# Moving GpSimd's hold for one DMA transpose, and the load of q of batch 5, ahead of a spectrum sum

## The chip, the cores and the metric

The kernel runs on one core of a Trainium2 chip. The metric is the device time of one execution in microseconds, lower being better. The kernel before was timed three times: 216.16, 216.46 and 216.47 us, with a median of 216.46 us.

## The reference, cut to what matters

Two layers follow each other. The first is linear attention without a softmax over 8 batches of 8 heads, 576 rows and 64 columns; the second is a gated long convolution, done with a Fourier transform over the 576 rows.

```python
kv  = einsum('bhsd,bhse->bhde', k, v)
o   = einsum('bhsd,bhde->bhse', q, kv)
x   = o / sqrt(mean(o * o, -1) + 1e-6) * g_norm     # heads side by side: [8, 576, 512]
x1, x2, x3 = split(x @ w_proj, 3, axis=-1)
conv = irfft(rfft(x2, axis=1) * rfft(filter_fft, axis=0), n=576, axis=1)
out = (x1 * conv * x3) @ w_out                      # [8, 576, 512] in float32
```

## The kernel before, in words

The kernel goes through the eight batches as a hand-written software pipeline. The string `ORDER` (lines 20 to 53) lists steps as `name.batch`; the loop at the end of the kernel calls them in that order, and each step appends its instructions to the queues of the engines it uses. Each engine (PE, the matmul engine; DVE, VectorE; ACT, ScalarE; POOL, GpSimd; SP, SyncE, which only issues DMAs) works through its own queue strictly in that order. Between engines a framework adds the waits that the data need: a step that writes a buffer waits for those that read its old content and a step that reads waits for the writer. So a word of `ORDER` that is moved changes the place of its instructions in the queue of its own engine, and nothing else in the code.

The steps that matter here, with their lines in the kernel before:

- `Lq.b`, `Lk.b`, `Lv.b` (line 121): one DMA each, issued by POOL, that loads q, k or v of batch b from memory, turning float32 into bfloat16, into one of two buffers (`qb`, `kb`, `vb`; batch b uses buffer b modulo 2). `Lq.5` writes the q buffer that batch 3 used.
- `Qt.b` (line 409): a DMA transpose, issued by SP, from the q buffer into `qT`, again one of two. It waits for the landing of `Lq.b`. Batches 2 to 7 use it; batches 0 and 1 are transposed on PE.
- `Qh.b` (line 413): a POOL copy of two elements of `qT` into a tile that nobody reads. It waits for the landing of `Qt.b`, and so holds whatever comes behind it in POOL's queue until then. This is the hold of the title.
- `K.b` and `eK.b` (lines 384 and 390): k times v on PE, and its copy out of PSUM by ACT. `O01.b` and `O23.b` (line 458): q times that product for two groups of heads each, on PE; they need `qT`. `sq`, `ob`, `R`, `rs`, `x0`, `x1` (lines 468, 475, 465, 479, 493): square, copy, sum of squares, reciprocal root, and the normalised x.
- `fd`, `fr`, `fa` (lines 504 to 518): sums and differences of thirds of x ahead of the Fourier transform, on DVE. `F0`, `F1`, `F2`: forward transform on PE. `M0`, `M1` (line 606): products with the filter's spectrum on DVE, from PSUM into a float32 buffer. `M2` (line 621): the same for the small third group. `A0`, `A1` (line 612): the spectrum sums on POOL, which add two halves of that float32 buffer into `Y`. In batches 0 and 7 DVE does one of them (`Av1`).
- `Io01`, `I01`, `Io23`, `I23` (lines 658 and 659): the inverse transform on PE from `Y`. Line 659 multiplies the part that `A0` writes.
- `Ga`, `Gb` (line 631): the projections for x1 and x3 on PE. `x1` followed by a second digit, as in `x12.3` (line 637), and `g` (line 639): their evictions, the second with the product x1 times x3.
- `U`, `ot` (lines 754 to 774): the output product, its copy by ACT into one of three tiles, and four DMAs to memory issued by SP.

PSUM is four pairs of banks. A matmul group takes the pair that has been free longest, and is held by the step that still has to evict it.

POOL's queue around the change is, in the order before: `Lv.4`, `Qh.3`, `A1.2`, `Lk.5`, `Lv.5`, `A0.2`, `Lq.5`, `Lk.6`, `Qh.4`, `A1.3`, `Lv.6`, `A0.3`, `Lq.6`, `Qh.5`. SP's queue is: the DMAs of `ot0.0`, `Qt.4`, those of `ot2.0`, `ot0.1` and `ot4.1`, `Qt.5`, those of `ot2.1`, `Qt.6`, those of `ot0.2`.

Of the kernel before, what the change touches and what calls it, by code (L numbers as in the profile page):

```python
# [28 lines left out]
F1t.1 A0.1 Ga3.1 rs1.2 M1.1 K.3 Gb3.1 x13.1 x1.2 eK.3 F2.1 O23.3 g3.1 F2t.1 Lq.4 sq3.3 Lk.4 M2.1 A1.1 sq2.3 U0.0  # L29
Io01.1 ob3.3 I01.1 x0.2 ob2.3 os01.1 ot0.0 Ga2.1 Io23.1 fd.2 x12.1 Ga1.2 u01.1 os23.1 fa.2 x11.2 I23.1 R3.3 Gb2.1  # L30
rs3.3 O01.3 sq0.3 u23.1 g2.1 ob0.3 abM.2 R0.3 Ga0.2 w.1 sq1.3 Lv.4 fr.2 ob1.3 abT.2 rs0.3 x10.2 eT.2 R1.3 fin.1 Gb1.2
eab.2 rrM.2 rs1.3 F1.2 R2.3 F1t.2 g1.2 rrT.2 rs2.3 F2.2 err.2 x0.3 Qh.3 K.4 Qt.4 eK.4 F2t.2 M1.2 A1.2 U2.0 x1.3 M2.2
Ga3.2 O23.4 ot2.0 x13.2 sq3.4 fr.3 Lk.5 F0.2 U0.1 sq2.4 ob3.4 Gb3.2 ob2.4 Gb0.2 Lv.5 M0.2 A0.2 fd.3 ot0.1 rrM.3 R2.4
rrT.3 g0.2 Ga2.2 g3.2 rs2.4 R3.4 err.3 Io01.2 x12.2 I01.2 os01.2 rs3.4 U4.1 Io23.2 fa.3 Gb2.2 u01.2 os23.2 I23.2 abM.3
Lq.5 ot4.1 abT.3 g2.2 x1.4 u23.2 eab.3 w.2 Ga0.3 eT.3 F1.3 O01.4 F1t.3 x10.3 U2.1 Qt.5 sq1.4 ob1.4 sq0.4 M1.3 Lk.6
Ga1.3 ob0.4 fin.2 ot2.1 F0.3 R0.4 x11.3 rs0.4 Qh.4 K.5 eK.5 F2.3 M0.3 A1.3 Gb0.3 R1.4 g0.3 F2t.3 M2.3 rs1.4 Ga2.3
x12.3 Gb2.3 O23.5 g2.3 sq3.5 ob3.5 Gb1.3 x0.4 Lv.6 A0.3 Ga3.3 g1.3 Io01.3 sq2.5 Lq.6 ob2.5 os01.3 x13.3 I01.3 fd.4
fa.4 u01.3 fr.4 U0.2 Io23.3 Qt.6 ot0.2 abT.4 eT.4 os23.3 Gb3.3 g3.3 O01.5 I23.3 abM.4 sq0.5 u23.3 w.3 Ga0.4 sq1.5
ob0.5 R3.5 ob1.5 eab.4 x10.4 K.6 F2.4 R2.5 rs3.5 eK.6 F2t.4 rs2.5 Qh.5 fin.3 rrM.4 R1.5 M2.4 rs1.5 F1.4 R0.5 F1t.4
# [842 lines left out]
```

## Time and profile before

| what | value |
|---|---|
| median of three runs | 216.46 us |
| the profiled execution, its own time | 218.23 us |
| span from first to last instruction in that execution | 216.5 us |
| PE busy | 200.6 us, 93% of the span |
| DVE busy | 182.6 us, 84% |
| ACT busy | 147.9 us, 68% |
| POOL busy | 70.6 us, 33% |
| granted PE clock, mean | 0.994 |

All times below are microseconds from the start of the span, in one profiled execution. A row of a timeline gives the start, the duration, the engine, the line of the kernel, the operation, the tiles written and read, the shapes and a count; in brackets stands the time that the engine sat idle before it, and what ended that. `SPq` is SP's queue. A DMA has two times: the time that its issuing engine was occupied, and the time from issue to landing, which another view gives in a row that ends with that number. In the table of windows each engine's busy time in a stretch stands with its count of instructions, and at the end of the row are the granted clock, the busy share of the DMA engines (1.00 is sixteen engines with one packet each) and the rate in GB/s.

### The profile page before, as it was taken

To read this page: it belongs to the slowest core of one execution; us is meant where nothing else is said; L and a number is where in the kernel's file an instruction comes from. 1 tells how busy PE (TensorE), PEld (TensorE's weight loads), DVE (VectorE), ACT (ScalarE), POOL (GpSimd) and SP (SyncE) were. 2 spreads that over 40 slices of the span, in tenths; PEclk is the share of its full clock that TensorE was granted. 3 is DMA by queue.
4 is the path that set the end of the run, shared out by engine and by line. 5 is a ranking of instruction groups with operands and counts; after the bars stand their busy time and mean duration, and the time that the engine had idled before them with its cause. 6 is when DMAs were issued, how large, how long until landed. Compare 5 with 4: busy or idle time off the path is not lost.

```text
span 216.5 us, 4609 instructions
## 1 busy us (share of the span) xinstructions
PE 200.6 (93%) x1852; PEld 122.0 (56%) x1852; DVE 182.6 (84%) x275; ACT 147.9 (68%) x232; POOL 70.6 (33%) x67
## 2 busy tenths in 40 slices
PE   4879999999999999999879999999999999999960
PEld 1544555574657555665555566656574586557620
DVE  7875888799999999989869977899988899998830
ACT  3688775989959888659567978677666863524430
POOL 8662001404294007702910047107600440042031
PEclk9999999999999999999999999999999999999997
DMA  3999999999969944999996903999340221102584
GB/s 41 201 211 204 207 202 204 172 197 166 203 84 196 201 89 81 189 233 175 142 241 109 152 3 88 168 236 182 88 117 0 76 74 41 56 3 74 121 208 133
DMA packets 40810, 30.12 MB, mean 139 GB/s; under 512 B 15796, under 2 KB 36276, under 8 KB 40788
## 3 DMA queue, kind: packets, MB, share of 16 engines
q0 software_dynamic: 21376, 17.63, 53.0%
q1 hardware_dynamic: 19172, 11.80, 26.4%
q10 hardware_dynamic: 240, 0.39, 0.7%
q8 instruction: 14, 0.23, 0.4%
q14 instruction: 8, 0.07, 0.1%
HBM read 33.69 MB, written 9.44 MB: 199 GB/s over the span
## 4 chain that ended last, share of the span: by engine, by line
PE 64%; DMA 11%; issue 8%; POOL 5%; ACT 5%; DVE 4%; POOLq 0%; DVEq 0%; ACTq 0%
PE ps L631 23%; PE ps L754 9%; DMA wp<-in_moe_w_proj_dram 7%; PE ps L548 6%; PE ps L658 4%; DMA qT<-qb 4%; PE ps L554 2%; PE ps L465 2%; DVE tpw L606 2%; PE ps L534 2%; PE ps L384 2%; PE ps L458 2%; POOL kb L121 2%; PE ps L580 1%; PE ps L573 1%
## 5 line engine op out<-in xcount | busy, mean ns | idle before, releaser
L612 POOL TENSOR_TENSOR Y<-tpw 97x1024 bf16<-97x1024 f32 (+1 forms) x14 | 38.8, 2773 | 109.5 <-DVE tpw L606 109.4
L631 PE MATMUL ps<-x,wp 128*128 128x288 bf16 x512 | 71.3, 286 | 1.3 <-DMA wp<-in_moe_w_proj_dram 0.5
L631 PEld LDWEIGHTS <-wp 128*128 128x128 bf16 x512 | 48.5, 98 | 19.7 <-issue 3.3
L606 DVE TENSOR_TENSOR tpw<-ps,HH 97x2048 f32<-97x2048 f32 (+1 forms) x16 | 36.6, 2287 | 3.4 <-PE ps L587 1.8
L639 DVE TENSOR_TENSOR g<-ps,x 128x576 bf16<-128x576 f32 x32 | 23.9, 753 | 7.0 <-PE ps L631 4.8
L479 ACT ACTIVATE rstd<-ps,bias_eps 128x576 bf16<-128x576 f32 x32 | 23.3, 745 | 6.5 <-PE ps L465 6.3
L637 ACT CAST x<-ps 128x576 bf16<-128x576 f32 x32 | 20.5, 644 | 10.5 <-PE ps L631 10.3
L754 PE MATMUL ps<-wo,yg 128*128 128x512 bf16 x112 | 26.3, 379 | 0.0
L558 ACT CAST x<-ps 128x1024 bf16<-128x1024 f32 (+1 forms) x24 | 20.4, 881 | 6.8 <-PE ps L548 3.3
L468 ACT ACTIVATE sq<-ps 128x576 bf16<-128x576 f32 x32 | 20.2, 661 | 5.4 <-PE ps L458 5.3
L475 ACT ACTIVATE o<-ps,g_col 128x576 bf16<-128x576 f32 x28 | 20.5, 758 | 0.0
L758 ACT COPY ot<-ps 128x1024 f32<-128x1024 f32 x13 | 13.2, 1016 | 7.6 <-PE ps L754 7.6
L754 PEld LDWEIGHTS <-yg 128*128 128x128 bf16 x112 | 10.6, 98 | 11.6 <-issue 0.5
L658 PE MATMUL ps<-IV,Y 128*128 128x192 bf16 x120 | 15.5, 245 | 0.0
L548 PE MATMUL ps<-wp,ab 128*128 128x512 bf16 x64 | 15.1, 379 | 0.0
L662 ACT COPY os<-ps 128x576 f32<-128x576 f32 x15 | 9.6, 639 | 7.8 <-PE ps L659 4.7
L493 DVE TENSOR_TENSOR x<-o,rstd 128x1152 bf16<-128x1152 bf16 x16 | 12.0, 755 | 2.9 <-ACT rstd L479 2.9
L667 DVE TENSOR_TENSOR u<-ps,os 128x576 bf16<-128x576 f32 x15 | 11.3, 754 | 3.3 <-ACT os L662 1.7
L465 PE MATMUL ps<-sq,ind 128*128 128x288 bf16 x64 | 12.8, 286 | 0.4 <-ACT kvblk L390 0.3
L659 PE MATMUL ps<-IV,Y 97*128 97x96 bf16 x60 | 12.4, 207 | 0.0
L621 DVE TENSOR_TENSOR Y<-ps,HM 128x1024 bf16<-128x1024 f32 x8 | 9.7, 1218 | 2.2 <-PE ps L598 2.2
L658 PEld LDWEIGHTS <-Y 128*128 128x128 bf16 x120 | 9.5, 98 | 3.6 <-issue 0.9
(167 smaller groups left out, 310.5 us busy)
## 6 DMA issues: line engine op xcount, KB each, us to landing
out_dram<-ot SPq DMA_DIRECT2D x54, 128.0 KB, 2.4
qb<-in_q_dram POOLq DMA_DIRECT2D x8, 576.0 KB, 7.3
kb<-in_k_dram POOLq DMA_DIRECT2D x7, 576.0 KB, 12.1
vb<-in_v_dram POOLq DMA_DIRECT2D x7, 576.0 KB, 9.5
wp<-in_moe_w_proj_dram POOLq DMA_DIRECT2D x3, 512.0 KB, 16.8
out_dram<-ot SPq DMA_DIRECT2D x12, 64.0 KB, 2.2
kb<-in_k_dram POOLq DMA_DIRECT2D x2, 288.0 KB, 7.7
vb<-in_v_dram POOLq DMA_DIRECT2D x2, 288.0 KB, 7.7
```

The costliest lines, as they stand in the source:

```text
L468: act.activation(out=halves(sq()[:, j]), in_=tmp['o', b, j][:, :, 0:TH], func=AF.Square)
L475: act.activation(out=by_time(osb(), j), in_=i_, func=AF.Copy, scale=g_col)
L479: act.activation(out=by_time(rstd(), j), in_=by_row(tmp['r', b, j]), func=AF.Abs_reciprocal_sqrt, scale=1.0 / D, bias=bias_eps)
L548: nc.tensor.matmul(pp[:, h], abt()[:, j, 2 * h * P:(2 * h + 1) * P], w2(j), start=(j == 0), stop=(j == NDC - 1))
L558: act.copy(out=o_(), in_=tmp[key, b])
L606: vec.tensor_mul(out=t_[:n], in0=xp[:n].unsqueeze(1).to_broadcast([n, 2, 2, DM]), in1=two)
L612: op(out=Yt()[:n, 2 * g:2 * g + 2], in0=t_[:n, ::-1, 0], in1=t_[:n, ::-1, 1])
L631: nc.tensor.matmul(pp[:, h, 0:TH], w_, x[:, j, h * TH:(h + 1) * TH], start=(j == 0), stop=(j == NDC - 1))
L637: act.copy(out=x1, in_=pp[:, :, 0:TH])
L639: vec.tensor_mul(out=halves(g13t()[:, dc]), in0=pp[:, :, 0:TH], in1=x1)
L658: nc.tensor.matmul(pp[:, i, 0:SB], Y[:, 2 * g + h, cs], IV[:, 2 * g + h, 0:SB], start=(g == 1), stop=(g == 2))
L754: nc.tensor.matmul(pp[:, cc], ygt(b)[:, dc, b % 2 * 64 + c * P:b % 2 * 64 + (c + 1) * P], wo[:, dc], start=(dc == 0), stop=(dc == NDC - 1))
```

## The change

Two words of `ORDER` are moved, and the words around them are re-wrapped into lines. `Qh.4` and `Lq.5` now stand directly ahead of `A1.2`, behind `M1.2`. Before, `Lq.5` stood behind `A0.2`, and `Qh.4` behind `Lk.6`. No instruction is added or removed, and no size is changed. POOL's queue becomes: `Lv.4`, `Qh.3`, `Qh.4`, `Lq.5`, `A1.2`, `Lk.5`, `Lv.5`, `A0.2`, `Lk.6`, `A1.3`, `Lv.6`, `A0.3`, `Lq.6`, `Qh.5`. The queues of the other engines stay as they are.

```diff
-eab.2 rrM.2 rs1.3 F1.2 R2.3 F1t.2 g1.2 rrT.2 rs2.3 F2.2 err.2 x0.3 Qh.3 K.4 Qt.4 eK.4 F2t.2 M1.2 A1.2 U2.0 x1.3 M2.2
-Ga3.2 O23.4 ot2.0 x13.2 sq3.4 fr.3 Lk.5 F0.2 U0.1 sq2.4 ob3.4 Gb3.2 ob2.4 Gb0.2 Lv.5 M0.2 A0.2 fd.3 ot0.1 rrM.3 R2.4
-rrT.3 g0.2 Ga2.2 g3.2 rs2.4 R3.4 err.3 Io01.2 x12.2 I01.2 os01.2 rs3.4 U4.1 Io23.2 fa.3 Gb2.2 u01.2 os23.2 I23.2 abM.3
-Lq.5 ot4.1 abT.3 g2.2 x1.4 u23.2 eab.3 w.2 Ga0.3 eT.3 F1.3 O01.4 F1t.3 x10.3 U2.1 Qt.5 sq1.4 ob1.4 sq0.4 M1.3 Lk.6
-Ga1.3 ob0.4 fin.2 ot2.1 F0.3 R0.4 x11.3 rs0.4 Qh.4 K.5 eK.5 F2.3 M0.3 A1.3 Gb0.3 R1.4 g0.3 F2t.3 M2.3 rs1.4 Ga2.3
+eab.2 rrM.2 rs1.3 F1.2 R2.3 F1t.2 g1.2 rrT.2 rs2.3 F2.2 err.2 x0.3 Qh.3 K.4 Qt.4 eK.4 F2t.2 M1.2 Qh.4 Lq.5 A1.2 U2.0
+x1.3 M2.2 Ga3.2 O23.4 ot2.0 x13.2 sq3.4 fr.3 Lk.5 F0.2 U0.1 sq2.4 ob3.4 Gb3.2 ob2.4 Gb0.2 Lv.5 M0.2 A0.2 fd.3 ot0.1
+rrM.3 R2.4 rrT.3 g0.2 Ga2.2 g3.2 rs2.4 R3.4 err.3 Io01.2 x12.2 I01.2 os01.2 rs3.4 U4.1 Io23.2 fa.3 Gb2.2 u01.2 os23.2
+I23.2 abM.3 ot4.1 abT.3 g2.2 x1.4 u23.2 eab.3 w.2 Ga0.3 eT.3 F1.3 O01.4 F1t.3 x10.3 U2.1 Qt.5 sq1.4 ob1.4 sq0.4 M1.3
+Lk.6 Ga1.3 ob0.4 fin.2 ot2.1 F0.3 R0.4 x11.3 rs0.4 K.5 eK.5 F2.3 M0.3 A1.3 Gb0.3 R1.4 g0.3 F2t.3 M2.3 rs1.4 Ga2.3
```

## The prediction

> **What bounds the kernel now.** I began with the head of the page: which engine is full, and how full.
>
> ```profile
> span 216.5 us, 4609 instructions
> PE 200.6 (93%) x1852; PEld 122.0 (56%) x1852; DVE 182.6 (84%) x275; ACT 147.9 (68%) x232; POOL 70.6 (33%) x67
> ```
>
> PE works for 93% of the span, so time is won where PE stands still, or not at all. The table of windows shows where it does (span of the stretch, then busy time of PE, PEld, DVE, ACT and POOL, the clock, the DMA share, GB/s).
>
> ```profile
> 80.00:85.00 5.00, 5.00 (x34) 2.53 (x34) 4.93 (x6) 4.06 (x9) 4.03 (x3) 1.00 0.20 45
> 105.00:110.00 5.00, 2.94 (x29) 1.89 (x28) 3.28 (x4) 1.45 (x3) 3.91 (x4) 1.00 1.30 158
> ```
>
> Between 105 and 110 PE is busy for 2.94 us of 5.00, at full clock; from 80 to 85 it is full, as in the stretches around. That first row also shows the DMA engines nearly empty between 80 and 85. The timelines of PE, DVE and ACT name the hole:
>
> ```profile
> 105.25 2.12 PE L631 MATMUL ps<-x,wp 128*128 128x288 bf16 x16
> 109.44 0.44 PE L458 MATMUL ps<-qT,kvblk 64*64 64x288 bf16 x8 [2.06 <-DMA qT<-qb]
> 109.43 0.14 PEld L458 LDWEIGHTS <-kvblk 64*64 64x64 bf16 x8 [2.37 <-DMA qT<-qb]
> 105.64 1.21 DVE L621 TENSOR_TENSOR Y<-ps,HM 128x1024 bf16<-128x1024 f32 x1
> 111.00 0.76 DVE L639 TENSOR_TENSOR g<-ps,x 128x576 bf16<-128x576 f32 x1 [2.09 <-PE ps L631]
> 109.93 0.65 ACT L468 ACTIVATE sq<-ps 128x576 bf16<-128x576 f32 x1 [2.86 <-PE ps L458]
> ```
>
> `O23.5` is the second row. PE is done with its work before at 107.37 (105.25 and 2.12) and stands for **2.06 us** until the transpose of batch 5, `Qt.5`, has landed. DVE and ACT stand behind PE for 2.09 and 2.86 us. Next, why the transpose is late: SP's waits, its timeline, the chain of work that ended last (third row: start, length) and a landing.
>
> ```profile
> SPq L409 <- DMA qb<-in_q_dram: 5.3, 1, 5.3
> 95.98 0.43 SPq L774 DMA_DIRECT2D out_dram<-ot  x1
> 101.79 7.60 DMA qT<-qb
> qb<-in_q_dram POOLq DMA_DIRECT2D x1, 576.0 KB, 11.0
> ```
>
> SP had issued its last output at 96.41 and then waited 5.3 us for a load of q. `Qt.5` left at 101.79 and landed 7.60 us later, at 109.39, which is when PE goes on. The load is `Lq.5`, by POOL's timeline:
>
> ```profile
> 80.97 2.80 POOL L612 TENSOR_TENSOR Y<-tpw 128x1024 bf16<-128x1024 f32 x1 [13.57 <-DVE tpw L606]
> 83.73 0.79 POOL L121 DMA_DIRECT2D kb<-in_k_dram  x1
> 84.51 0.77 POOL L121 DMA_DIRECT2D vb<-in_v_dram  x1
> 87.72 3.00 POOL L612 TENSOR_TENSOR Y<-tpw 97x1024 bf16<-97x1024 f32 x1 [2.44 <-DVE tpw L606]
> 90.67 0.79 POOL L121 DMA_DIRECT2D qb<-in_q_dram  x1
> ```
>
> The rows are `A1.2`, `Lk.5`, `Lv.5`, `A0.2`, `Lq.5`. With its 11.0 us `Lq.5` lands at 101.67, just ahead of `Qt.5`. So the stall of PE hangs on a load that is issued late, behind `A0.2`, and travels behind two other loads.
>
> **The change part by part.** *The load.* `Lq.5` goes ahead of `A1.2`. What `Qt.4`, and so the hold, allows:
>
> ```profile
> 71.06 5.29 SPq L409 DMA_TRANSPOSE qT<-qb  x1
> qT<-qb SPq DMA_TRANSPOSE x1, 8.9
> L413 POOL COPY one__102<-qT x6: 174/243/920, 48.8 to 209.7; 1x2 bf16<-1x2 bf16 x6
> 109.51 0.17 POOL L413 COPY one__102<-qT 1x2 bf16<-1x2 bf16 x1 [0.77 <-DMA qT<-qb]
> 49.34 0.77 POOL L121 DMA_DIRECT2D kb<-in_k_dram  x1 [0.23 <-issue]
> ```
>
> `Qt.4` lands at 79.96 (71.06 and 8.9). POOL has been idle for a long time then (13.57 us before `A1.2`). `Qh.5` began 0.12 us after its landing, so `Qh.4` begins at 80.08, takes the median 0.24 us, and with the gap of 0.23 us that stood behind `Qh.2` the load is issued at 80.55 instead of 90.67, some 10 us earlier. It meets empty DMA engines. Its landing is bounded by its own 11.0 us, beside two loads, from above: 91.6, which is 4.9 us before SP asks for it at 96.41.
>
> *The transpose.* `Qt.5` can then leave at 96.4 or 96.5. How long it takes is not shown at that place; the six transposes bound it (second row; the third is `Qt.6`, and the first the packets of POOL's loads between 71 and 72, MB and share):
>
> ```profile
> q0 software_dynamic: 187, 0.14, 105.3%
> DMA to landing us min/median/max: 4.9/6.0/8.9
> qT<-qb SPq DMA_TRANSPOSE x1, 5.9
> ```
>
> I take 8.9, that of `Qt.4`, the nearest: it left while 187 packets of loads passed in its first microsecond, as `Qt.5` will after the change, behind outputs of SP too. That is a landing at 105.4, 2.0 us before PE comes at 107.37; with 4.9 it is 101.4. The other conditions of `O23.5` are met by then: its PSUM pairs are freed by `rs1.4` and by `M2.3`, the row of line 621 above, which ends at 106.85. So the whole stall goes: **minus 2.06 us**. `A1.3`, whose start at 101.48 lies just ahead of `Qt.5`, can't be a condition of it, since it comes later in `ORDER`.
>
> *The hold.* This is the cost. `A1.2` now stands behind `Qh.4` and the issue of `Lq.5`: 80.55 and 0.79 give 81.34 as its start, 0.37 later than its 80.97. What hangs on it:
>
> ```profile
> 80.80 0.75 DVE L493 TENSOR_TENSOR x<-o,rstd 128x1152 bf16<-128x1152 bf16 x1
> 105.65 2.36 POOL L612 TENSOR_TENSOR Y<-tpw 97x1024 bf16<-97x1024 f32 x1
> 82.60 1.59 DVE L509 TENSOR_TENSOR x<-x 128x768 bf16<-128x768 bf16 x1
> 114.93 0.55 DVE L509 TENSOR_TENSOR x<-x 128x768 bf16<-128x768 bf16 x1
> 85.36 2.28 DVE L606 TENSOR_TENSOR tpw<-ps,HH 97x2048 f32<-97x2048 f32 x1
> 90.86 0.21 PE L659 MATMUL ps<-IV,Y 97*128 97x96 bf16 x1
> ```
>
> A sum on POOL undisturbed takes 2.36 us (second row). `A1.2` took 2.80 while DVE ran `x1.3` until 81.55 (first row); ending at 83.77, it did its real work from 81.41. DVE's next instruction with two SBUF inputs, `fr.3`, took 1.59 us instead of 0.55 and ended 0.42 us after `A1.2`. So the two exclude each other, and the end of `A1.2` does set something: `fr.3`, then DVE without a gap to `M0.2` at 85.36, then `A0.2`, which ends at 90.72 just before PE reads its result at 90.86. A delay of the end of `A1.2` would reach PE whole. But a start at 81.34 is before 81.41, within the time that `x1.3` covers: the cost is 0. If `Qh.4` takes the longest 0.92 us, the start is 82.02 and the cost 0.6; it is not below nothing, since `x1.3` stays where it is. I take **0** and keep 0.6.
>
> *The loads behind it.* `Lk.5` and `Lv.5` keep their place in time but now travel behind 576 KB more.
>
> ```profile
> vb<-in_v_dram POOLq DMA_DIRECT2D x1, 576.0 KB, 13.5
> 102.62 0.95 PE L384 MATMUL ps<-vb,kb 96*64 96x64 bf16 x48
> ```
>
> `Lv.5` landed at 98.0 (84.51 and 13.5), `K.5` reads it at 102.62. As third of three loads it lands at the latest where the third landed before, 101.67, and with the head start of 3.2 us (80.55 against 83.73) at about 98.5, an estimate from these rows. Cost 0; the cover is 0.9 to 4.1 us. `Lk.6` is issued in the place that `Lq.5` leaves, and is needed a batch later. `Qh.4` at its old place had nothing to wait for.
>
> *What is late next.* `Lq.6` is still issued at 107.95, behind `A0.3`, so `Qt.6` doesn't move with PE:
>
> ```profile
> SPq L409 <- DMA qb<-in_q_dram: 7.7, 1, 7.7
> 116.22 2.90 SPq L409 DMA_TRANSPOSE qT<-qb  x1
> 127.44 0.44 PE L458 MATMUL ps<-qT,kvblk 64*64 64x288 bf16 x8
> ```
>
> `Qt.6` lands at 122.1 (116.22 and its 5.9, from the row above). `O23.6` at 127.44 comes to 125.4: 3.3 us are left. `A0.3`, issued at 105.65 and done at 108.0, is needed by the inverse transform of batch 3; that stands behind `O23.5` and sixteen matmuls of line 631, which took 2.12 us above, so not before 109.8 after the change. DVE and ACT stood still beside PE and move with it. So nothing takes the gain back that I can see.
>
> **Sum.** The profiled execution took 218.23 us; without 2.06 it is 216.2. It lies 1.77 above the median of the runs, 216.46; the same saving there gives **214.4 us**.
>
> **The rivals.** *The shared transpose.* `Qt.5` now runs beside the last load of k instead of after it. If it gets half of the engines to its end, twice the 5.9 us of `Qt.6` make 11.8: landing at 108.3, `O23.5` 1.1 earlier instead of 2.06: 215.3 us. For it: `Qt.4`, 3.0 us above `Qt.6`. Against it: even `Qt.4` took 8.9, and the loads should run out about 3 us earlier than at present. By the Trainium skill ("DMA: Bandwidth & Descriptors", section "SWDGE vs HWDGE vs iDMA") every DMA engine takes turns between the queues fed by software and by hardware. By that rule alone the result would be this rival's; the trace agrees only in part, by the 3.0 us.
>
> *The longer hold.* `Qh.4` takes 0.92 us, or the transpose of batch 4 lands a little later: 0.6 us reach PE at 90.9 and the gain is 1.5: 215.0 us. What made the longest copy long:
>
> ```profile
> 66.48 0.92 POOL L413 COPY one__102<-qT 1x2 bf16<-1x2 bf16 x1
> 66.40 0.96 DVE L504 TENSOR_TENSOR d__517<-x 128x1536 bf16<-128x1536 bf16 x1
> ```
>
> It ran beside a DVE instruction with two SBUF inputs, as `A1.2` beside `x1.3`. Against this rival: at 80.1 DVE is in `M1.2`, whose other input is PSUM, and `x1.3` begins only at 80.80.
>
> *The starved product, slower.* The loads might give way to `Qt.5`. If `Lv.5` comes in only when `Qt.5` lands, at 105.4, `K.5` starts 2.8 us late, and everything on PE behind it; against the 2.06 that is 0.7 slower than before: 217.2 us. It decides from a landing of `Lv.5` at 104.7 (102.62 and 2.06). For it is that `Lq.5` goes ahead of `Lv.5`; against it, that `Lv.5` would have to land 6 us later than my estimate.
>
> *No effect.* `Qt.5` leaves early and PE gains nothing, because `O23.5` or something soon behind it waits for another thing until the old time: 216.5. For it, only that waits behind the last one don't show; against it are the conditions gone through above.
>
> **How the numbers follow.** A measurement of this kernel tells some 0.2% from no change, 0.4 us. Forecast 0.66, shared transpose 0.09, longer hold 0.08, all three faster by over 0.2%: 0.83. No effect 0.06. Starved product, and the slower side of what I have missed: 0.11. The range begins at 213.7: the 2.37 us for which PE's weight load waited at the same place instead of 2.06, and 0.3 for the spread of the runs (216.16 to 216.47). It ends at 215.9, above both smaller gains with a like margin, and leaves out the last two cases.
>
> **What would show it.** Right: a q load at about 80.6 ahead of the sum of line 612; that sum ending near 83.8; `Qt.5` issued near 96.5 and landed before 107; no idle time in front of the product of line 458 near 107.4; PE full from 105 to 110. Wrong: the sum ending at 84.2 or later and the inverse transform late at 90.9 (hold); `Qt.5` landing after 107.4 (sharing); `K.5` waiting for a load at 102.6 (starving); or a new idle time of PE behind 110, first of all at `O23.6`.

## The result, and the profile after

The change makes no difference that can be told. Twenty executions of the changed kernel have a median of 216.51 us (215.96 to 218.09), twenty of the kernel before 216.42 us (216.09 to 217.71). The ratio after to before is 1.0006, with a 95% interval of 0.9992 to 1.0019. The forecast was 214.4 us, 2.06 us less. It was wrong. Medians cover all executions of a kernel; ratios, here and below, leave out those that took over 1.5% more than its fastest: none here, but three of the kernel before (220.15 to 220.72 us), two of each kernel with memsets and one of the kernel with two loads ahead.

The profile of the changed kernel looks, at the place of the change, just as the forecast wanted it. First the head of the page and the row of the windows from 105 to 110:

```profile
span 215.9 us, 4607 instructions
105.00:110.00 5.00, 5.00 (x54) 3.37 (x48) 4.27 (x5) 3.16 (x8) 4.99 (x4) 1.00 0.76 134
```

PE is full where it had been busy for 2.94 us of 5.00. The timelines of POOL, SP and PE, with the landings of `Lq.5` and `Qt.5` (the rows that end in 6.1 and 5.9):

```profile
79.21 0.17 POOL L413 COPY one__102<-qT 1x2 bf16<-1x2 bf16 x1 [10.24 <-DMA qT<-qb]
79.69 0.77 POOL L121 DMA_DIRECT2D qb<-in_q_dram  x1 [0.30 <-issue]
qb<-in_q_dram POOLq DMA_DIRECT2D x1, 576.0 KB, 6.1
82.54 2.80 POOL L612 TENSOR_TENSOR Y<-tpw 128x1024 bf16<-128x1024 f32 x1 [2.08 <-DVE tpw L606]
85.29 0.79 POOL L121 DMA_DIRECT2D kb<-in_k_dram  x1
98.15 3.83 SPq L409 DMA_TRANSPOSE qT<-qb  x1
qT<-qb SPq DMA_TRANSPOSE x1, 5.9
106.83 2.12 PE L631 MATMUL ps<-x,wp 128*128 128x288 bf16 x16
108.88 0.44 PE L458 MATMUL ps<-qT,kvblk 64*64 64x288 bf16 x8
```

`Lq.5` leaves at 79.69 and lands at 85.8. `Qt.5` leaves at 98.15, right behind SP's outputs, and lands at 104.05. `O23.5` follows the matmuls before it without idle time. `A1.2` still takes 2.80 us and waits for DVE, not for the hold.

One more thing must be read before the two spans are compared. From about 17 us on, everything in this execution is late. The sum of batch 1 on POOL, long before the change, in the kernel before and then in the changed one:

```profile
57.93 3.40 POOL L612 TENSOR_TENSOR Y<-tpw 97x1024 bf16<-97x1024 f32 x1 [6.29 <-DVE tpw L606]
```

```profile
59.51 3.40 POOL L612 TENSOR_TENSOR Y<-tpw 97x1024 bf16<-97x1024 f32 x1 [6.40 <-DVE tpw L606]
```

That is 1.58 us, in code that is the same in both. By ACT's rows, what starts at 16.6 in the kernel before starts 0.33 us later in this execution, what starts at 18.3 starts 1.8 us later, and what starts at 24 starts 1.57 us later. The windows of the changed kernel show what stands there (the granted clock is the third number from the end):

```profile
16.00:18.00 2.00, 1.89 (x12) 0.51 (x11) 1.59 (x3) 2.00 (x4) 0.77 (x1) 0.70 1.28 199
18.00:20.00 2.00, 2.00 (x19) 0.76 (x20) 1.30 (x2) 0.13 (x1) 0.00 (x0) 0.50 1.28 205
```

PE's clock was granted at 0.70 and 0.50 between 16 and 20 in this execution, and at 1.00 in the kernel before. Two stretches of 2 us at 0.70 and 0.50 lack 1.6 us of full clock, which is about the delay. Taken off its span of 215.9, the 1.58 us leave 214.3; the span of the kernel before, 216.5, less its stall of 2.06 is 214.4. So between these two executions the change did what was forecast of it. The medians say that it does nothing of the kind in most executions. That is what the experiments had to explain.

### The profile page after: what moved, and what is told of

Read it like the earlier page. It is cut to its first block, busy times and chain, and to the rows that moved or that the text cites. A ratio compares the mean times of both kernels' runs of the same rounds, so it can differ in the third digit from the quotient of the medians.

```text
span 215.9 us, 4607 instructions
## 1 busy us (share of the span) xinstructions
PE 202.4 (94%) x1852; PEld 122.4 (57%) x1852; DVE 183.0 (85%) x275; ACT 148.1 (69%) x232; POOL 70.7 (33%) x67
## 4 chain that ended last, share of the span: by engine, by line
PE 81%; ACT 8%; DMA 4%; DVE 3%; POOL 1%; issue 1%; POOLq 0%; DVEq 0%; ACTq 0%
PE ps L631 27%; PE ps L754 11%; PE ps L548 7%; PE ps L658 5%; DMA vb<-in_v_dram 4%; PE ps L554 3%; PE ps L465 3%; PE ps L384 3%; PE ps L534 2%; PE ps L458 2%; PE ps L580 2%; ACT rstd L479 2%; PE ps L573 2%; PE ps L541 2%; PE ps L767 1%; PE ps L793 1%
```

## The experiments

**Theory 1**: the stall of 2.06 us belongs to the one execution that was profiled; most executions of the kernel before have none worth naming, so there is nothing to remove. **Theory 2**: the stall is in every execution, and the changed kernel gives its 2 us back somewhere. Ratios are to the kernel before, timed beside. In the diffs of `ORDER` only the words around the change stand; `...` marks what is cut from a line.

### The kernel before, profiled twice more

No edit.

> The kernel before, profiled once more, nothing changed. Theory 1 (the stall of 2.06 us at O23.5 belongs to the one execution that was profiled; most executions of the kernel before have a short stall there or none): idle time of PE before the first O of batch 5 under 0.7 us, a span near 214.7 us. Theory 2 (the stall is in every execution, and the changed kernel gives its 2 us back somewhere else): a stall of 1.8 to 2.3 us, Qt.5 issued some 5 us after SP's last output, while the span is again near 214.7 or 216.5.

> The same kernel before a second time. Theory 1: again under 0.7 us of idle time of PE before the first O of batch 5. Theory 2: again about 2 us. If the two repeats disagree, the stall varies from execution to execution, and neither theory is right in its plain form.

The spans were 214.5 and 214.8 us, the times 216.33 and 216.54 us. From the first repeat, PE's, POOL's and SP's timelines, with the landings of `Lv.5`, `Lq.5` and `Qt.5`:

```profile
105.44 2.12 PE L631 MATMUL ps<-x,wp 128*128 128x288 bf16 x16
107.50 0.44 PE L458 MATMUL ps<-qT,kvblk 64*64 64x288 bf16 x8
84.70 0.78 POOL L121 DMA_DIRECT2D vb<-in_v_dram  x1
vb<-in_v_dram POOLq DMA_DIRECT2D x1, 576.0 KB, 11.9
90.86 0.79 POOL L121 DMA_DIRECT2D qb<-in_q_dram  x1
qb<-in_q_dram POOLq DMA_DIRECT2D x1, 576.0 KB, 9.4
100.37 3.50 SPq L409 DMA_TRANSPOSE qT<-qb  x1
qT<-qb SPq DMA_TRANSPOSE x1, 6.7
```

From the second:

```profile
105.54 2.12 PE L631 MATMUL ps<-x,wp 128*128 128x288 bf16 x16
107.72 0.44 PE L458 MATMUL ps<-qT,kvblk 64*64 64x288 bf16 x8
100.88 3.58 SPq L409 DMA_TRANSPOSE qT<-qb  x1
qT<-qb SPq DMA_TRANSPOSE x1, 6.8
```

There is no stall. The load took 9.4 us (9.8 in the second) instead of 11.0, the transpose 6.7 and 6.8 instead of 7.6. The transpose landed at 107.07 in the first, 0.4 us before `O23.5` began, and at 107.68 in the second, when `O23.5` began at 107.72. So the transpose is not early in the kernel before: in these two executions it lands within half a microsecond of the moment at which PE asks for it. Theory 1 fits, and theory 2 has nothing to give back.

The rows also take the first profile one step further back. `Lv.5`, the load ahead of `Lq.5`, landed at 96.60 here, at 97.10 in the second repeat (12.3 us) and at 98.01 in the first profile (13.5 us). `Lq.5` landed 3.66 us behind it in all three. So its 11.0 us against 9.4 and 9.8 are the lateness of `Lv.5`, handed on.

### Batch 5's load of q left out

```diff
-Lq.5 ot4.1 abT.3 g2.2 ...
+ot4.1 abT.3 g2.2 ...
```

> The kernel before without Lq.5: batch 5 works on the q of batch 3, so that Qt.5 waits for no load and can leave as soon as SP has issued its outputs; the load's traffic is missing too. Theory 1 (no stall in most executions): the time stays within 0.4 us of the kernel before, 216.0 to 216.8. Theory 2 (2 us of stall in every execution): 1.5 to 2.3 us faster, 214.1 to 214.9, since no hold and no load stand in the way that could give it back.

216.43 us, ratio 0.9984 (0.9963 to 1.0005). Taking the whole load away gains 0.2% at the most likely, and 0.4% at the end of the interval. Theory 2, which needed 0.7 to 1.1%, is out: no stall of 2 us stands in the median execution.

### The load alone moved, without the hold

```diff
-... M1.2 A1.2 U2.0 ...
+... M1.2 Lq.5 A1.2 U2.0 ...
-Lq.5 ot4.1 abT.3 g2.2 ...
+ot4.1 abT.3 g2.2 ...
```

> The kernel before with Lq.5 alone moved ahead of A1.2; Qh.4 stays at its old place, so that POOL doesn't wait for the transpose of batch 4 and the load leaves near 68 us. Theory 1: within 0.4 us of the kernel before. Theory 2 with the hold as what gives the gain back: 1.5 to 2.2 us faster. Theory 2 with the earlier load traffic as what gives it back: within 0.4 us, but with the stall at O23.5 gone in its profile and a new idle time of PE or a slower transpose of batch 4 elsewhere.

216.49 us, ratio 0.9986 (0.9968 to 1.0004): nothing again. The profile shows what the hold is for. The load, the transpose of batch 4 and its first user:

```profile
67.40 0.77 POOL L121 DMA_DIRECT2D qb<-in_q_dram  x1
qb<-in_q_dram POOLq DMA_DIRECT2D x1, 576.0 KB, 13.1
71.26 7.51 SPq L409 DMA_TRANSPOSE qT<-qb  x1
qT<-qb SPq DMA_TRANSPOSE x1, 12.1
83.42 0.44 PE L458 MATMUL ps<-qT,kvblk 64*64 64x288 bf16 x8 [0.33 <-DMA qT<-qb]
```

The load leaves at 67.40, the transpose of batch 4 meets it and takes 12.1 us, where it took 6.2 to 8.9 in all the other profiles, and `O23.4` waits 0.33 us for it.

### The hold alone moved

```diff
-... M1.2 A1.2 U2.0 ...
+... M1.2 Qh.4 A1.2 U2.0 ...
-... rs0.4 Qh.4 K.5 ...
+... rs0.4 K.5 ...
```

> The kernel before with Qh.4 alone moved ahead of A1.2; Lq.5 stays behind A0.2. Theory 1 (the hold is hidden in POOL's idle time, since the transpose of batch 4 lands at 80.0 or earlier and the sum can't run before 81.4): the time within 0.4 us of the kernel before. Theory 2, the part that puts the loss on the hold: 0.6 us or more slower, with the sum of line 612 starting later than DVE's product ends.

Ratio 1.0010 (0.9979 to 1.0041), median 216.99 us against 216.60: not told from nothing, with a wide interval. In POOL's timeline the hold ends before DVE has finished what the sum needs:

```profile
77.54 0.17 POOL L413 COPY one__102<-qT 1x2 bf16<-1x2 bf16 x1 [10.17 <-DMA qT<-qb]
80.93 2.81 POOL L612 TENSOR_TENSOR Y<-tpw 128x1024 bf16<-128x1024 f32 x1 [3.22 <-DVE tpw L606]
```

So for neither part by itself a difference can be told, with up to 0.4% left open for the hold. Three of the ten executions of this kernel, in which the load is still late, lay above 217.4 us; more of that below.

### The sum twice: what a longer hold would cost

```diff
-... M1.2 Qh.4 Lq.5 A1.2 U2.0
+... M1.2 Qh.4 Lq.5 A1.2 A1.2 U2.0
```

> The changed kernel with A1.2 issued twice (the second adds the same halves into the same place), so that the end of that sum moves by 2.4 us with nothing else moved ahead or back. If the end of the sum reaches PE whole through fr.3, M0.2, A0.2 and the inverse transform of batch 2, as the prediction put it: 2.0 to 2.6 us slower than the kernel before, 218.4 to 219.1 us. If there is slack on that path: up by less than 1 us, and the price of a longer hold in the prediction was too high.

218.28 us, ratio 1.0073 (1.0047 to 1.0099): 1.6 us more, 1.0 to 2.1, where I had expected 2.0 to 2.6. The timelines of POOL, DVE and PE:

```profile
79.90 0.17 POOL L413 COPY one__102<-qT 1x2 bf16<-1x2 bf16 x1 [12.48 <-DMA qT<-qb]
80.38 0.77 POOL L121 DMA_DIRECT2D qb<-in_q_dram  x1 [0.31 <-issue]
81.16 5.26 POOL L612 TENSOR_TENSOR Y<-tpw 128x1024 bf16<-128x1024 f32 x2
84.24 2.60 DVE L511 TENSOR_TENSOR x<-x,x 128x768 bf16<-128x768 bf16 x1
87.42 2.28 DVE L606 TENSOR_TENSOR tpw<-ps,HH 97x2048 f32<-97x2048 f32 x1
89.76 1.02 PE L534 MATMUL ps<-wp,rr 128*128 128x512 bf16 x4 [1.87 <-DVE tpw L606]
```

The first three rows are also a picture of the hold as it was forecast: hold from 79.90, load issued at 80.38, sum from 81.16. The end of POOL's sums came 2.6 us later than in the profile before (86.42 against 83.77). DVE's first instruction of `fr.3` slipped in between the two sums; its second waited, 2.60 us in all; `M0.2` came at 87.42 instead of 85.36, 2.06 us late, and PE stood 1.87 us. So the path from the end of that sum to PE is tight: of 2.65 us, 1.87 us reach PE in this execution, some 70%, and 1.6 us the time. It is not the whole that was forecast, and PE stands earlier than forecast, at line 534, which waits for `M0.2`, and not at the inverse transform of line 659. In the changed kernel this path isn't touched.

By the Trainium skill ("SBUF — State Buffer", section "Who interferes with whom") a DVE instruction with two SBUF inputs and a GpSimd instruction that reads SBUF exclude each other, and the one that comes second waits until the first has ended. The 2.60 us of the second instruction of `fr.3`, which took 0.56 us in the kernel before and here ended 0.42 us after the sums, agree.

### The load of q later, by one load and by two

```diff
-Lq.5 ot4.1 abT.3 g2.2 ...
+Lk.6 Lq.5 ot4.1 abT.3 g2.2 ...
-... sq0.4 M1.3 Lk.6
+... sq0.4 M1.3
```

The second kernel has `Lk.6 Lv.6 Lq.5` there, and no `Lv.6` behind `x0.4`.

> The kernel before with Lk.6 issued ahead of Lq.5 (they swap places behind A0.2), so that the load of q of batch 5 lands where that of k of batch 6 landed, some 3.0 us later (103.2 against 100.3 in the first repeat of the kernel before). Theory 1, made sharper (in most executions Qt.5 lands within half a microsecond of the moment PE asks for it, 107.1 against 107.5 in one repeat and 107.7 against 107.7 in the other): a stall of 2.0 to 3.0 us before the first O of batch 5, and the time up by as much, 218.3 to 219.5 us. Rival (in most executions the transpose has microseconds to spare, and the stall in the first profile was a rare accident on an otherwise idle path): up by less than 0.5 us.

> As the one with Lk.6 ahead, and Lv.6 ahead of Lq.5 too: two loads of 576 KB more in front of it, some 6 us. Theory 1, made sharper: a stall of 4.5 to 6 us and the time up by as much, 220.9 to 222.5 us, so that each load in front costs its whole 2.5 to 3 us. Rival (microseconds to spare): up by 3 us less than that.

223.42 us, ratio 1.0327 (1.0252 to 1.0402), and 227.05 us, 1.0437 (1.0359 to 1.0514). The sign fits the sharper theory, that the transpose lands within half a microsecond of the moment PE asks for it, and excludes a path with microseconds to spare. The sizes don't: I had expected 2 to 3 us for the first and 4.5 to 6 for the second, and they took 6.8 and 10.5 us more in the median. The first one's transpose, the stall and the windows behind it:

```profile
103.98 3.52 SPq L409 DMA_TRANSPOSE qT<-qb  x1
112.58 0.69 PE L458 MATMUL ps<-qT,kvblk 64*64 64x288 bf16 x8 [4.57 <-DMA qT<-qb]
112.00:114.00 2.00, 1.42 (x12) 0.72 (x13) 0.00 (x0) 0.67 (x2) 0.17 (x1) 0.50 1.18 252
114.00:116.00 2.00, 2.00 (x12) 1.35 (x11) 0.65 (x1) 1.78 (x3) 0.00 (x0) 0.64 1.22 260
```

The transpose left 3.1 us later than in the second repeat and took 1.8 us more (8.6): a stall of 4.57 us. Behind it PE got its clock only at 0.50 and 0.64, and the same eight matmuls of line 458 take 0.69 us instead of 0.44. The span is 220.9, 6.1 above that of the second repeat: 0.3 by which this execution had been late before, the stall, and 1.2 us behind it, where the clock was low.

### A small delay: one and two memsets ahead of the load

```diff
+    pad_ = consts.tile([P, 1024], BF16)
+
+    @one
+    def Pd(b):
+        nc.gpsimd.memset(pad_, 0.0)
...
-Lq.5 ot4.1 abT.3 g2.2 ...
+Pd.5 Pd.5 Lq.5 ot4.1 abT.3 g2.2 ...
```

The first kernel has one `Pd.5`. Lines behind 404 have moved by 5.

> The kernel before with one POOL memset of 128 by 1024 bfloat16 elements (0.95 us by the row of line 303) into a tile that nobody reads, between A0.2 and Lq.5: the load of q of batch 5 is issued 0.95 us later, and nothing else is changed but the load of k behind it. If in most executions the transpose lands within half a microsecond of the moment PE asks for it: 0.4 to 1.0 us slower than the kernel before, 216.9 to 217.5 us. If there is more to spare: within 0.3 us.

> The same with two memsets, 1.9 us. If the transpose lands on the edge: 1.3 to 2.0 us slower, 217.8 to 218.5 us, with a stall of that size at the first O of batch 5 and PE at full clock behind it, so that a stall of 2 us costs 2 us and the further loss with the swapped loads (4.57 us of stall, 6 us of span) comes from the lower clock behind the longer stall. If there is more to spare: under 1 us.

With one: 216.91 us, ratio 1.0014 (0.9996 to 1.0032), not told from nothing; the profiled execution has its transpose at 107.75 (issued at 101.15, 6.6 us) and no stall to speak of. With two: 217.76 us for all ten and 217.47 for the eight that the ratio counts, 1.0039 (1.0016 to 1.0061). That is 0.3 to 1.3 us, under the 1.3 to 2.0 us that I had expected, so a delay of the issue doesn't reach PE whole. A part of it is lost before the landing: in the profile with one memset `Lq.5` was issued 1.0 us later than in the two repeats and landed 0.3 and 0.8 us later, at 101.03. How much room the edge has in most executions is therefore not shown. From the profiled execution with two, its page's head, POOL's and PE's timelines and two landings:

```profile
span 216.5 us, 4587 instructions
84.74 0.77 POOL L121 DMA_DIRECT2D vb<-in_v_dram  x1
vb<-in_v_dram POOLq DMA_DIRECT2D x1, 576.0 KB, 13.5
92.79 0.79 POOL L121 DMA_DIRECT2D qb<-in_q_dram  x1
qb<-in_q_dram POOLq DMA_DIRECT2D x1, 576.0 KB, 9.1
109.42 0.44 PE L463 MATMUL ps<-qT,kvblk 64*64 64x288 bf16 x8 [1.82 <-DMA qT<-qb]
```

This is the profile of the kernel before over again: a stall of 1.82 us, a span of 216.5 us, a time of 218.23 us, and PE's clock at 1.00 behind it. But the trace doesn't show that the memsets made it. `Lv.5` took 13.5 us, as in the first profile, and landed at 98.24; `Lq.5` landed at 101.89, the same 3.65 us behind it as without memsets. That the memsets slow the kernel rests on the ratio.

### The changed kernel again

No edit to the changed kernel.

> The changed kernel again, timed beside the kernel before. If what the change takes away is the stall of those executions in which Qt.5 lands late: the median within 0.4 us of the kernel before, and none of its runs above 217.4 us at a mean granted clock of 0.985 or more, where so far 10 of some 70 runs of kernels with the late load are, and none of 42 with the early one. If those slow runs have another cause: one or two of twelve above 217.4 us here too.

216.39 us (215.94 to 216.67), ratio 0.9995 (0.9982 to 1.0007). The profiled execution has a span of 214.4 us. POOL's sum, DVE's `M0.2`, PE's `O23.5`, and the issues and landings of the last load of k and of `Qt.5`:

```profile
81.03 2.80 POOL L612 TENSOR_TENSOR Y<-tpw 128x1024 bf16<-128x1024 f32 x1 [0.20 <-DVE tpw L606]
85.43 2.28 DVE L606 TENSOR_TENSOR tpw<-ps,HH 97x2048 f32<-97x2048 f32 x1
107.37 0.44 PE L458 MATMUL ps<-qT,kvblk 64*64 64x288 bf16 x8
90.74 0.80 POOL L121 DMA_DIRECT2D kb<-in_k_dram  x1
kb<-in_k_dram POOLq DMA_DIRECT2D x1, 576.0 KB, 10.4
96.64 4.61 SPq L409 DMA_TRANSPOSE qT<-qb  x1
qT<-qb SPq DMA_TRANSPOSE x1, 6.7
```

The load left at 80.06 here, and the sum still waited for DVE and not for the hold. `M0.2` begins 0.07 us later than in the first profile, as the sum of batch 1 does (58.00 against 57.93): the hold cost nothing here. `O23.5` begins without idle time.

None of the twelve lies above 217.4 us. Over all experiments, of the 68 timed executions of the kernel before that the ratios count 7 lay above 217.4 us at a mean clock of 0.985 or more; of 56 of kernels with the load early or absent none did (two did at clocks of 0.982 and 0.979, the first of them the profiled one above). That fits a change that takes away a rare stall. Beside these twelve, though, it was 1 of 26, and the limit was chosen when the other counts were known. Only one such execution of the kernel before has a trace, so it isn't shown for the others.

## Why the prediction was wrong, by its own steps

- **What bounds the kernel.** Read rightly for the execution that was profiled, down to the load as the cause; why that load was late lies further back, in `Lv.5` ahead of it. Not right for the kernel: the repeats have no such stall.
- **The load and the transpose.** Right. The load was issued at 79.69, which is 78.1 with the 1.58 taken off, against the 80.55 of the forecast, since the transpose of batch 4 took 6.4 us instead of 8.9. `Qt.5` left when SP was free and took 5.9 us (6.7 in the repeat), below the 8.9 that I had chosen.
- **The shared transpose**, a rival: its price was not paid. `Qt.5` ran beside the last load of k (issued at 92.25, landed after 9.5 us at 101.75) for 3.6 of its 5.9 us, and in the repeat for 4.5 of its 6.7. Over the five profiles of kernels in which the load of q is early or absent, the time of `Qt.5` rises with the time from its issue to the landing of that load: 2.1, 3.2, 3.6, 4.5 and 4.7 us went with 5.1, 5.6, 5.9, 6.7 and 6.9 us. But `Qt.6`, in whose time no packet of POOL's loads runs, took 5.9 us in the first profile of either kernel, so how much of this is the load's doing isn't shown. The rival's 11.8 us are far off, since it let the load run beside the transpose to its end; the slowest of the five landed 3.8 us before PE asked. The Trainium skill's rule, named there, that the engines take turns between the queues doesn't say how much that costs.
- **The hold.** Cost 0 is right. The price of a longer one was put too high: a delay of the sum's end was to reach PE whole, and 1.87 of 2.65 us did.
- **The loads behind it, and what is late next.** Right: in the two profiles of the changed kernel no wait of PE for k, v or q appears behind the change.
- **The sum.** This is the step that failed, and in one sentence: "It lies 1.77 above the median of the runs, 216.46; the same saving there gives 214.4 us." The profiled execution took 218.23 us because it had the stall. The 1.77 us by which it lay above the median were that stall, and I then subtracted its 2.06 us from the median, which doesn't contain it. 218.23 less 2.06 is 216.2, a few tenths from the median of either kernel. The saving holds for that execution and those like it; the two other profiles of the kernel before, both near the median, have no stall, and without the load at all the median gains 0.4% at the end of the interval.
- **No effect**, the rival that came true, had 0.06, and the reason that I gave for it (PE waits for another thing) was not the one. What I lacked was the rival that the stall itself varies: its length is the landing of the transpose less the moment at which PE asks for it, and that landing was 109.39 in the first profile against 107.07 and 107.68 in the repeats, 1.7 to 2.3 us, about as much as the stall measured.

What stays open is why `Lv.5`, and with it `Lq.5`, was late in the first profiled execution, by 0.9 to 1.4 us, why the transpose was 0.8 to 0.9 us slower there, and how often this happens in executions without a trace. A transpose that leaves later runs for longer beside `Lv.6`, whose issue (104.84) doesn't move with it; that would lengthen it further, but no run tests this by itself.

## What to carry to other kernels

When the profiled execution lies above the median by about the size of the stall that a change removes, the first thing to suspect is that the excess is the stall: compare its time with the whole distribution before subtracting, and look at a second profile. A wait for a DMA is not a constant like the duration of a matmul; ask by how much its landing scatters, and whether the landing is normally just in time. Moving a transfer that lands just in time can only help the rare execution in which it is late; here it brought nothing that can be told to the median.

## What the runs showed of the hardware that was not expected

A stall of PE of 1.82 or 2.06 us left its clock at 1.00. Longer ones did not. Beside the rows from 112 to 116 above, of the kernel with one load ahead, stand these of the kernel with two, in which PE stood for 8.86 us:

```profile
110.00:112.00 2.00, 0.00 (x0) 0.00 (x0) 0.00 (x0) 0.00 (x0) 0.00 (x0) 0.76 1.14 163
120.00:122.00 2.00, 2.00 (x17) 1.54 (x16) 1.97 (x4) 0.12 (x1) 0.00 (x0) 0.68 0.94 189
```

If the clock within a row is either 1.00 or 0.50, it fell at 112.0 and 111.0, 4.0 and 3.1 us after PE had run dry (108.0 and 107.9), and came back at 115.4 and 121.3, 2.9 and 4.5 us after PE had gone on (112.58 and 116.77). By the Trainium skill ("TensorE: Matmul & The Clock Gate", section "What's actually happening") the clock falls to half after an idle window of about 3.4 us and comes back after as long a busy one. The traces agree with that roughly, within about a microsecond on both sides. The low clock is a part of why the load that was one place later cost 6.8 us in the median and not 3.

The same clock was granted at 0.50 to 0.70 between 16 and 20 us in one execution of the changed kernel and at 1.00 in the other twelve that were profiled; that execution was some 1.6 us late from then on, and no run here shows why.

Two facts on DMAs. Of two loads of 576 KB in one queue the second landed 3.66 us behind the first in three executions, though its time from issue to landing went from 9.4 to 11.0 us: what a load waits for in its queue is in that time. And a DMA transpose is not of one length: that of batch 5 took 5.1 to 6.9 us in the five profiles compared above, the longer the load beside it still ran, and that of batch 4 took 6.2 and 8.2 us in two executions in which a load of v ran beside it for 3.3 us in both.
